# Raw weights of groups 2 to 4 land in buffers of the units, the first six state products are copied to C and A, and the list of operations is ordered anew

## The chip, the cores and the metric

The kernel runs on one core of a Trainium2 chip. The metric is the device time of one launch in microseconds. Three runs of the kernel before gave 668.93, 672.35 and 676.08 us, a median of 672.35 us. One more execution was profiled: 671.54 us, of which 669.7 us are the span from the first instruction to the last; all times of the trace count from the start of that span.

## The reference

The program is cross attention between tokens and a small state, followed by a feed-forward layer with a rational activation. The weights arrive as float64.

```python
# x [8, 8, 512, 64], state [8, 8, 32, 64]
a = softmax(scale * x @ state.T);      xread = a @ state
a2 = softmax(scale * state @ x.T);     sread = a2 @ x
x = concat([xread, sread])             # to 8 * 544 rows of 512
h = x @ w_in                           # w_in [512, 2048], float64
P = a[0] + a[1] * h + a[2] * h**2 + a[3] * h**3
Q = 1.0 + abs(b[0]) * abs(h) + abs(b[1]) * h**2
out = (P / (Q + 1e-06)) @ w_out        # w_out [2048, 512], float64
```

## The kernel before

**Tiling.** The 2048 hidden columns are cut into 8 blocks u of 256. A step n is one batch b = n // 8 and one block u = n % 8; steps 0 to 63 cover the eight batches, steps 64 to 71 the state rows. For the batches the kernel does not compute x @ w_in: it multiplies the state with w_in first (a state product), and step n then multiplies that product m with the transposed softmax aT. TensorE therefore needs, for step n, the product m of its batch and block.

**State products.** X:i (i = 4u + e, 32 of them) multiplies block u of w_in with the states of batches 2e and 2e + 1, on TensorE, into one of two PSUM buffers of two banks (tag `h`, shared with the h of the steps and with the attention of batches 1 to 7). XA:i (ScalarE) or XV:i (VectorE) copies the result out of PSUM into a tile of the tag `xo`, of which there are two; XS:i stores that tile to a scratch tensor in HBM. For batch 0 the product is not stored but split at once into a high part (fh, ScalarE) and a low part (fo, VectorE). For the later batches lm:n loads a pair of products back and fs:n splits each (ScalarE, then GpSimd).

**Weights.** 16 groups k in the order in0, in1, in2, out0, in3, out1, in4, out2, ...; each is 1 MB of float64 in two halves of 512 KB, the size of most transfers here. lr:i (i = 2k + j) loads half j of group k into a tile of the tag `raw`, which has two tiles of two halves: the halves of group k + 2 wait until group k has been read. cp:k (ScalarE) and jr:k (VectorE) take the two 32-bit words of each number apart, jl:k (VectorE) joins them to float32. An "in" group becomes a tile win of block u (three buffers), stored with jw:u for later; an "out" group is split by sp:k (ScalarE, then GpSimd) into the resident w_out.

**A step.** F:n:0 and F:n:1 (TensorE, 6 matmuls each) make h in PSUM. FC:n and FB:n (ScalarE) write C and A from it; mu, po, qd (VectorE) read h again, qa, ln, ex (ScalarE) make the reciprocal L; g1, g2, g3 (VectorE) and gl (GpSimd) or gv (VectorE) make the high and low part gh and gl. mh:n:t (4 matmuls) and ml:n:t (2 matmuls) multiply them with w_out for row block t. C and A have three buffers each, L, gh and gl two each.

**What sets the order.** A list ORDER of some 2200 tokens. Each engine, and SyncE (SP) which issues all loads and stores, executes its tokens strictly in the order in which they stand in the list; a token waits only for its data and its buffers, and everything behind it on its engine waits with it. Attention of a batch (scores, row_T, row_max, row_sub, row_exp, row_sum, row_eps, row_norm, a_T, a_hi, a_lo; col_max, col_scale, col_exp, e2_T, sread and so on) stands in the same list. Names that end in p (row_sup, a_lp) are the GpSimd form of the same operation, those in v (row_norv) the VectorE form.

The lines that the change touches are `load_raw` (L271 to L285), `conv_parts` and `join_rest` (L287 to L311), `extra_out` (L615 to L619) and ORDER.

Of the kernel before, what the change touches and what calls it, by code (L numbers as in the profile page):

```python
# [9 lines left out]
F32 = mybir.dt.float32  # L10
F32R = mybir.dt.float32r
I32 = mybir.dt.int32
U32 = mybir.dt.uint32
# [5 lines left out]
P = 128  # L19
# [169 lines left out]
def attention_rational_ffn(  # L189
# [9 lines left out]
    S = 2 * xT.shape[4]  # L199
# [744 lines left out]
```

## Time and profile before

| what | value |
|---|---|
| median of three runs | 672.35 us (668.93 to 676.08) |
| profiled execution | 671.54 us |
| its span | 669.7 us |
| TensorE (PE) busy | 643.5 us |
| VectorE (DVE) busy | 624.2 us |
| ScalarE (ACT) busy | 515.8 us |
| GpSimd (POOL) busy | 318.3 us |
| mean granted TensorE clock | 0.989 of 2.4 GHz |

Busy time is the union of an engine's instructions. The span is best read in three pieces: the first 134 us, in which the weights are loaded, converted and multiplied with the state beside the eight steps of batch 0; the 519 us of the later steps; and the last 17 us.

### The profile page before, as it was taken

How to read it: one execution, taken by the hardware profiler on the slowest of the kernel's cores; microseconds unless marked ns; L12 is line 12 of the kernel's file. 1: busy time of each engine (PE TensorE's matmuls, PEld its weight loads, DVE VectorE, ACT ScalarE, POOL GpSimd, SP SyncE). 2: the span in 40 equal slices, each digit the busy share in tenths (PEclk: the TensorE clock that was granted, in tenths of full speed). 3: DMA queues.
4: the chain of work that ended last, by engine and by line, in shares of the span. 5: the costliest groups of instructions: out<-in, count | busy, mean ns of one | idle time of the engine just before them, and what ended most of it. 6: DMA issues, size and time to landing. Idle time of an engine off the chain costs nothing.

```text
span 669.7 us, 11219 instructions
## 1 busy us (share of the span) xinstructions
PE 643.5 (96%) x4474; PEld 512.9 (77%) x4474; DVE 624.2 (93%) x593; ACT 515.8 (77%) x611; POOL 318.3 (48%) x172
## 2 busy tenths in 40 slices
PE   6769989999999999999999999999999999999997
PEld 3445556778887888788887888788878888888995
DVE  5889999999999999999999999999999899999885
ACT  4689898887877887787868787797787678865663
POOL 1105255355454566545554545555446446465541
PEclk8989999999999999999999999999999999999999
DMA  7889987615112422213223132231225101211301
GB/s 298 310 315 335 331 329 257 226 54 178 44 34 93 136 77 96 69 26 105 85 101 120 71 89 69 79 142 32 95 79 174 32 1 47 64 47 60 100 1 63
DMA packets 28984, 81.46 MB, mean 122 GB/s; under 512 B 2820, under 2 KB 2948, under 8 KB 28932
## 3 DMA queue, kind: packets, MB, share of 16 engines
q1 hardware_dynamic: 28932, 80.75, 35.1%
q8 instruction: 35, 0.57, 0.3%
q14 instruction: 17, 0.14, 0.1%
HBM read 52.95 MB, written 27.79 MB: 121 GB/s over the span
## 4 chain that ended last, share of the span: by engine, by line
PE 88%; DMA 5%; ACT 3%; DVE 2%; issue 1%; SPq 1%; ACTq 0%
PE h L696 28%; DMA m_dram<-xo 3%; PE ps_x L607 3%; PE o__5754 L769 2%; PE o__3525 L769 2%; PE o__1763 L769 2%; PE o__2310 L769 2%; PE o__4679 L769 2%; PE o__4049 L769 2%; PE o__2879 L769 2%; PE o__3495 L769 2%; PE o__5233 L769 2%; PE o__2341 L769 2%; PE o__5794 L769 2%; PE o__4054 L769 2%; PE o__5172 L769 2%
## 5 line engine op out<-in xcount | busy, mean ns | idle before, releaser
L759 POOL TENSOR_TENSOR gl<-C,L 128x1024 fp32r<-128x1024 f32 (+1 forms) x70 | 174.1, 2487 | 230.4 <-DVE C L752 174.0
L696 PE MATMUL h<-aT,m 128*128 128x512 f32 x768 | 191.3, 396 | 4.2 <-DVE xo L619 4.1
L696 PEld LDWEIGHTS h<-aT,m 128*128 128x128 f32 x768 | 144.9, 190 | 38.5 <-issue 3.5
L708 ACT ACTIVATE C<-h,cst 128x1024 f32<-128x1024 f32 (+1 forms) x72 | 83.3, 1157 | 44.6 <-PE h L696 32.1
L656 POOL TENSOR_TENSOR m<-m_sb,m 128x512 fp32r<-128x512 f32 x56 | 79.9, 1432 | 60.3 <-ACT m L655 40.0
L715 ACT ACTIVATE A<-h,cst 128x1024 f32<-128x1024 f32 (+1 forms) x72 | 76.7, 1066 | 29.2 <-PE h L696 26.9
L740 DVE SCALAR_TENSOR_TENSOR gh<-C,cst,L 128x1024 fp32r<-128x1024 f32 (+1 forms) x72 | 91.8, 1274 | 6.2 <-ACT L L811 2.6
L729 DVE SCALAR_TENSOR_TENSOR A<-A,b0a,h 128x1024 f32<-128x1024 f32 (+1 forms) x72 | 87.5, 1216 | 9.4 <-ACT A L715 7.2
L752 DVE SCALAR_TENSOR_TENSOR C<-C,cst,A 128x1024 f32<-128x1024 f32 (+1 forms) x72 | 88.8, 1233 | 2.2
L723 DVE SCALAR_TENSOR_TENSOR C<-C,cst,h 128x1024 f32<-128x1024 f32 (+1 forms) x72 | 87.8, 1219 | 2.1
L746 DVE SCALAR_TENSOR_TENSOR A<-A,gh 128x1024 f32<-128x1024 f32 (+1 forms) x72 | 88.0, 1222 | 1.6
L735 ACT ACTIVATE A<-A 128x1024 f32<-128x1024 f32 (+1 forms) x72 | 72.7, 1012 | 19.2 <-DVE A L729 19.1
L719 DVE TENSOR_TENSOR C<-C,h 128x1024 f32<-128x1024 f32 (+1 forms) x72 | 82.9, 1152 | 3.9 <-ACT C L708 2.4
L801 ACT ACTIVATE L<-A 128x1024 f32<-128x1024 f32 (+1 forms) x72 | 73.0, 1013 | 3.4 <-POOL gl L759 0.3
L811 ACT ACTIVATE L<-L 128x1024 f32<-128x1024 f32 (+1 forms) x72 | 72.9, 1014 | 1.5
L607 PE MATMUL ps_x<-win_sb,st 64*32 64x256 f32 x1024 | 36.3, 403 | 15.2 <-DVE win_sb L320 6.3
L607 PEld LDWEIGHTS ps_x<-win_sb,st 64*32 64x32 f32 x1024 | 17.8, 111 | 30.9 <-ACT xo L619 10.5
L655 ACT CAST m<-m_sb 128x512 fp32r<-128x512 f32 x56 | 33.9, 614 | 0.0
L619 ACT COPY xo<-ps_x 128x1024 f32<-128x1024 f32 (+1 forms) x26 | 23.8, 933 | 5.0 <-PE ps_x L607 2.8
L332 POOL TENSOR_TENSOR wo<-cv_r,wo 128x1024 fp32r<-128x1024 f32 x7 | 16.9, 2410 | 17.6 <-ACT wo L331 17.6
L696 PEld LDWEIGHTS h<-sh,m 128*128 128x128 f32 x192 | 24.2, 191 | 0.7
L696 PE MATMUL h<-sh,m 128*128 128x256 f32 x192 | 24.4, 283 | 0.0
(254 smaller groups left out, 1113.2 us busy)
## 6 DMA issues: line engine op xcount, KB each, us to landing
m_sb<-m_dram SPq DMA_DIRECT2D x28, 512.0 KB, 4.5
m_dram<-xo SPq DMA_DIRECT2D x24, 512.0 KB, 4.2
out_dram<-o_sb SPq DMA_DIRECT2D x34, 256.0 KB, 4.3
xT_sb<-in_xT_dram SPq DMA_DIRECT2D x16, 512.0 KB, 5.1
raw<-in_w_in_dram SPq DMA_DIRECT2D x16, 512.0 KB, 6.4
raw<-in_w_out_dram SPq DMA_DIRECT2D x16, 512.0 KB, 5.6
x_sb<-in_x_dram SPq DMA_DIRECT2D x16, 512.0 KB, 7.0
w_in_dram<-win_sb SPq DMA_DIRECT2D x8, 512.0 KB, 5.4
```

Of the source, the lines that this page charges most:

```text
L656: nc.gpsimd.tensor_tensor(m[:, 1], t, m[:, 0].bitcast(F32), op=ALU.subtract)
L696: nc.tensor.matmul(h[:, ci * W : (ci + 1) * W], l, r, start=(q == 0), stop=(q == len(seq) - 1),)
L708: nc.scalar.activation(e["C"], e["h"], AF.Identity, scale=cst[:, 3:4], bias=cst[:, 2:3])
L715: nc.scalar.activation(e["A"], e["h"], AF.Abs, scale=cst[:, 5:6])
L719: nc.vector.tensor_tensor(e["C"], e["C"], e["h"], op=ALU.mult)
L723: nc.vector.scalar_tensor_tensor(e["C"], e["C"], cst[:, 1:2], e["h"], op0=ALU.add, op1=ALU.mult)
L729: nc.vector.scalar_tensor_tensor(e["A"], e["A"], b0a, e["h"], op0=ALU.add, op1=ALU.mult)
L740: nc.vector.scalar_tensor_tensor(e["gh"], e["C"], cst[:, 0:1], e["L"], op0=ALU.add, op1=ALU.mult)
L746: nc.vector.scalar_tensor_tensor(e["A"], e["A"], 1.0 + 1e-6, e["gh"].bitcast(F32), op0=ALU.add, op1=ALU.mult)
L752: nc.vector.scalar_tensor_tensor(e["C"], e["C"], cst[:, 0:1], e["A"], op0=ALU.add, op1=ALU.subtract)
L759: eng.tensor_tensor(e["gl"], e["C"], e["L"], op=ALU.mult)
L769: nc.tensor.matmul(O[t], e[l][:, j * W + t * P : j * W + (t + 1) * P], wo[:, k, 2 * u + j, :], start=(place == FIRST[n // U, t] and i + j ...
```

## The change

Three things. First, the raw halves of groups 2, 3 and 4 (halves 4 to 9) land in tiles of the tags gl, gh and L, which no step uses yet, and not in `raw`. Second, the first six state products (X:0 to X:5) are copied to tiles of the tags C and A (three each), and not to `xo`. Third, ORDER is another list of nearly the same tokens.

```diff
+    EARLY = {2: "gl", 3: "gh", 4: "L"}
+    XEARLY = {0: "C", 1: "C", 2: "C", 3: "A", 4: "A", 5: "A"}
+    BUFS = {"C": 3, "A": 3, "L": 2, "gh": 2, "gl": 2}
+
+    def spare(tag, dtype):
+        return ew.tile([P, 2 * S], dtype, name="spare", tag=tag, bufs=BUFS[tag])
+
...
-        if i // 2 not in RAW:
-            RAW[i // 2] = cv.tile([P, 2, 2 * CW, 2], U32, name="raw", tag="raw", bufs=2)
-        r = RAW[i // 2][:, j]
+        k = i // 2
+        if k in EARLY:
+            RAW[k, j] = spare(EARLY[k], U32).rearrange("p (f w) -> p f w", w=2)
+        elif (k, 0) not in RAW:
+            t = cv.tile([P, 2, 2 * CW, 2], U32, name="raw", tag="raw", bufs=2)
+            RAW[k, 0], RAW[k, 1], RAW[k, None] = t[:, 0], t[:, 1], t
+        r = RAW[k, j]
...
-        t = XO[i] = ew.tile([P, 2, 2, CW], F32, name="xo", tag="xo", bufs=2)
+        if i in XEARLY:
+            t = spare(XEARLY[i], F32).rearrange("p (q j f) -> p q j f", q=2, j=2)
+        else:
+            t = ew.tile([P, 2, 2, CW], F32, name="xo", tag="xo", bufs=2)
+        XO[i] = t
```

Of the list, one line of each start:

```diff
-    "warm:8 lt:0:0 ls:0:2 lt:0:1 scores:0:0 lc scores:0:1 cb b0a row_T:0:0 row_max:0:0 row_sub:0:0 lr:1 "
+    "lt:0:0 warm:8 ls:0:2 scores:0:0 lt:0:1 lc lr:1 cp:0:1 lr:0 cp:0:0 scores:0:1 row_T:0:0 jr:0:1 "
```

Some tokens change their form. The conversion of groups 2, 3 and 4 (cp, jr) goes half by half. From VectorE to GpSimd go row_sub of batches 0 (first half) and 1, row_norm of batch 0 (second half) and of batch 7 (first half), and a_lo of batches 0 (first half), 1 and 7; to VectorE goes row_norm of batch 2 (second half). XV, the VectorE form of the copy, is used for products 5, 13, 16, 26, 30, 31 and no longer for 4, 5, 11, 12, 20, 27. Of the low parts of the last steps, gl:66 and gl:68 become gv and gv:69 becomes gl.

**SP, from the first weights on** (raw and spare: weights on their way in; xo and, in the change, some spare tiles to m_dram: state products on their way out; win_sb: converted blocks of w_in; x_sb: the tokens). Before:

```order
L277 DMA raw<-in_w_in_dram 128x1024 x2
L252 DMA st<-in_stT_dram 128x768
L277 DMA raw<-in_w_in_dram 128x1024 x2
L283 DMA raw<-in_w_out_dram 128x1024 x2
L624 DMA m_dram<-xo 128x512
L624 DMA m_dram<-xo 128x1024 x2
L277 DMA raw<-in_w_in_dram 128x1024 x2
L624 DMA m_dram<-xo 128x1024
L352 DMA x_sb<-in_x_dram 128x1024
L624 DMA m_dram<-xo 128x1024
L277 DMA raw<-in_w_in_dram 128x1024
```

With the change:

```order
L288 DMA raw<-in_w_in_dram 128x1024 x4
L253 DMA st<-in_stT_dram 128x768
L288 DMA spare<-in_w_in_dram 128x1024
L294 DMA spare<-in_w_out_dram 128x1024 x2
L288 DMA spare<-in_w_in_dram 128x1024
L644 DMA m_dram<-spare 128x1024 x2
L288 DMA spare<-in_w_in_dram 128x1024 x2
L644 DMA m_dram<-spare 128x512
L341 DMA w_in_dram<-win_sb 128x1024
L644 DMA m_dram<-spare 128x1024
L294 DMA raw<-in_w_out_dram 128x1024 x2
L288 DMA raw<-in_w_in_dram 128x1024
```

Eight weight halves now stand ahead of the first product store, where four stood whose buffers were free and two that waited for one; the loads of x_sb stand later, behind further stores.

**VectorE, from the copy of X:5 to the first elementwise operations of step 0 and 1** (L619 or L639: the copies XV; L304 or L320 and the line after: jr and jl of a group; L636 or L656: fo; L719, L723, L729 or L739, L743, L749: mu, po, qd). Before:

```order
L619 COPY xo<-ps_x 128x2x2x256
L304 TENSOR_SCALAR cv_r<-raw 128x1024
L320 SCALAR_TENSOR_TENSOR cv_r<-cv_y,cv_r 128x1024
L636 TENSOR_TENSOR m<-ps_x,m 128x512
L475 TENSOR_SCALAR r_217<-r_217 128x2
L619 COPY xo<-ps_x 128x512
L304 TENSOR_SCALAR cv_r<-raw 128x1024
L320 SCALAR_TENSOR_TENSOR win_sb<-cv_y,cv_r 128x1024
L719 TENSOR_TENSOR C<-C,h 128x1024
L729 SCALAR_TENSOR_TENSOR A<-A,b0a,h 128x1024
L723 SCALAR_TENSOR_TENSOR C<-C,cst,h 128x1024
L729 SCALAR_TENSOR_TENSOR A<-A,b0a,h 128x1024
```

With the change:

```order
L639 COPY spare<-ps_x 128x2x2x256
L442 TENSOR_SCALAR cm<-cm 128x1 x2
L320 TENSOR_SCALAR cv_r<-spare 128x512 x2
L336 SCALAR_TENSOR_TENSOR win_sb<-cv_y,cv_r 128x1024
L320 TENSOR_SCALAR cv_r<-spare 128x512
L656 TENSOR_TENSOR m<-ps_x,m 128x512
L320 TENSOR_SCALAR cv_r<-spare 128x512
L749 SCALAR_TENSOR_TENSOR A<-A,b0a,h 128x1024
L320 TENSOR_SCALAR cv_r<-spare 128x512
L336 SCALAR_TENSOR_TENSOR cv_r<-cv_y,cv_r 128x1024
L739 TENSOR_TENSOR C<-C,h 128x1024
L743 SCALAR_TENSOR_TENSOR C<-C,cst,h 128x1024
```

The second copy of this stretch (XV:4) has left VectorE, group 2 is joined ahead of group 3, and the halves of group 3 fill the places between the operations of step 0.

## Rows read from the trace of the kernel before

**Rows 1.** The page, busy time of each engine, its share of the span, and its instructions.

```profile
PE 643.5 (96%) x4474; PEld 512.9 (77%) x4474; DVE 624.2 (93%) x593; ACT 515.8 (77%) x611; POOL 318.3 (48%) x172
```

**Rows 2.** Stretches of the span: from:to and length in us, busy us of each engine with its instructions, then the granted TensorE clock, the share of DMA time that was busy, and GB/s moved.

```profile
0.00:16.75 16.75, 10.46 (x138) 6.37 (x146) 8.93 (x17) 7.88 (x15) 2.80 (x8) 0.80 0.80 298
16.75:33.50 16.75, 11.78 (x152) 7.81 (x136) 13.79 (x21) 11.51 (x16) 3.28 (x2) 0.91 0.90 310
33.50:50.25 16.75, 11.32 (x212) 7.62 (x211) 14.26 (x16) 14.26 (x18) 1.40 (x2) 0.88 0.90 316
50.25:67.00 16.75, 15.25 (x204) 9.96 (x203) 15.34 (x14) 15.69 (x18) 9.28 (x4) 1.00 0.91 337
67.00:83.75 16.75, 15.68 (x245) 9.74 (x251) 15.62 (x17) 13.82 (x16) 3.33 (x2) 1.00 0.92 329
...
134.00:653.00 519.00, 519.00 (x2910) 427.73 (x2909) 498.03 (x452) 401.43 (x470) 272.24 (x145) 1.00 0.24 77
```

**Rows 3.** The chain that ended last, in order of time, from 0 to 140 us: start, length, what the chain went through. A DMA piece runs from its issue to its landing.

```profile
21.27 7.37 DMA m_dram<-xo
...
31.36 7.62 DMA m_dram<-xo
...
109.45 8.74 DMA x_sb<-in_x_dram
```

**Rows 4.** SP in order of time: start, length (of the issuing), line, what is moved.

```profile
4.39 0.94 SPq L277 DMA_DIRECT2D raw<-in_w_in_dram  x2
10.51 0.80 SPq L283 DMA_DIRECT2D raw<-in_w_out_dram  x2
...
19.10 1.15 SPq L277 DMA_DIRECT2D raw<-in_w_in_dram  x2
```

**Rows 5.** VectorE in order of time: start, length, line and operation; in brackets the idle time before it and what ended it.

```profile
7.60 0.72 DVE L441 STREAM_TRANSPOSE e<-ps_sc__109 128x512 f32<-128x512 f32 x1 [6.62 <-PE ps_sc__110 L402]
8.35 0.69 DVE L458 TENSOR_REDUCE mx<-e 128x16 f32<-128x512 f32 x1
9.07 0.69 DVE L466 TENSOR_TENSOR e<-e,mx 128x512 f32<-128x512 f32 x1
9.68 0.76 DVE L304 TENSOR_SCALAR cv_r<-raw 128x512 int32<-128x512 uint32 x2
10.56 1.23 DVE L320 SCALAR_TENSOR_TENSOR win_sb<-cv_y,cv_r 128x1024 int32<-128x1024 int32 x1
...
17.66 1.23 DVE L320 SCALAR_TENSOR_TENSOR win_sb<-cv_y,cv_r 128x1024 int32<-128x1024 int32 x1
...
22.31 1.21 DVE L619 COPY xo<-ps_x 128x1024 f32<-128x1024 f32 x1
...
28.67 0.69 DVE L619 COPY xo<-ps_x 128x512 f32<-128x512 f32 x1 [2.30 <-DMA m_dram<-xo]
...
33.53 1.28 DVE L723 SCALAR_TENSOR_TENSOR C<-C,cst,h 128x1024 f32<-128x1024 f32 x1
...
51.42 1.28 DVE L729 SCALAR_TENSOR_TENSOR A<-A,b0a,h 128x1024 f32<-128x1024 f32 x1 [1.75 <-ACT C L708]
```

**Rows 6.** TensorE in order of time, in the same columns. Each F of a step is one row x12 (steps 0, 1, 2, 3, 5 and 9 here), each X one row x32, each mh one row x4.

```profile
11.84 3.67 PE L607 MATMUL ps_x<-win_sb,st 64*32 64x256 f32 x64 [4.01 <-DVE win_sb L320]
...
23.57 3.04 PE L696 MATMUL h<-aT,m 128*128 128x512 f32 x12 [1.18 <-DVE xo L619]
29.51 4.49 PE L696 MATMUL h<-aT,m 128*128 128x512 f32 x12 [2.90 <-DVE xo L619]
34.95 1.10 PE L607 MATMUL ps_x<-win_sb,st 64*32 64x256 f32 x32 [0.95 <-DVE C L723]
...
44.76 4.37 PE L696 MATMUL h<-aT,m 128*128 128x512 f32 x12
48.97 1.07 PE L769 MATMUL o__573<-wo,gh 128*128 128x512 f32 x4
49.88 1.07 PE L769 MATMUL o__580<-wo,gh 128*128 128x512 f32 x4
50.88 1.09 PE L607 MATMUL ps_x<-win_sb,st 64*32 64x256 f32 x32
51.91 1.20 PE L769 MATMUL o__621<-wo,gh 128*128 128x512 f32 x4
...
58.32 3.03 PE L696 MATMUL h<-aT,m 128*128 128x512 f32 x12
...
91.38 3.01 PE L696 MATMUL h<-aT,m 128*128 128x512 f32 x12
...
134.79 2.88 PE L696 MATMUL h<-aT,m 128*128 128x512 f32 x12
```

**Rows 7.** GpSimd in order of time, in the same columns: row_sub and a_lo of a half of batch 0.

```profile
15.03 1.05 POOL L466 TENSOR_TENSOR e<-e,mx 128x512 f32<-128x512 f32 x1 [0.17 <-DVE mx L458]
22.54 1.27 POOL L522 TENSOR_TENSOR aT<-eT,aT 128x512 fp32r<-128x512 f32 x1 [6.46 <-ACT aT L518]
```

**Rows 8.** Groups of instructions of the first 140 us, shapes apart: line, engine, operation, shapes and count; busy us, mean ns of one; idle before them in us, and what ended it. XA of a whole product, cp of half a group, FC.

```profile
L619 ACT COPY xo<-ps_x 128x1024 f32<-128x1024 f32 x21 | 20.8, 1015 | 2.6 <-DMA m_dram<-xo 1.3 <-PE ps_x L607 0.8 <-ACT cv_y L294 0.4
...
L708 ACT ACTIVATE C<-h,cst 128x1024 f32<-128x1024 f32 x10 | 12.1, 1206 | 3.5 <-PE h L696 3.4
...
L294 ACT ACTIVATE cv_y<-raw 128x512 f32<-128x512 f32 x4 | 2.7, 673 | 0.7 <-DMA raw<-in_w_in_dram 0.6
```

More of the change, by code (lines that the diff above doesn't have):

```diff
@@ L263, in attention_rational_ffn @@
             groups.append(("in", u + 3))
-    NU = 2 * len(groups)
+    EARLY = {2: "gl", 3: "gh", 4: "L"}
[3 more added lines that the diff above has]
+        return ew.tile([P, 2 * S], dtype, name="spare", tag=tag, bufs=BUFS[tag])
     RAW, CV, win_t = {}, {}, {}
@@ L285, in load_raw, with raw_words @@
             )
+    def raw_words(k, j, w):
+        if j is None:
+            return RAW[k, None][:, :, :, w]
+        return RAW[k, j][:, :, w].unsqueeze(1)
     def conv_parts(k, j=None):
@@ L295, in conv_parts @@
             CV[k][0][:, js].bitcast(F32),
-            RAW[k][:, js, :, 1].bitcast(F32),
+            raw_words(k, j, 1).bitcast(F32),
             AF.Prelu,
@@ L305, in join_rest @@
             CV[k][1][:, js],
-            RAW[k][:, js, :, 0],
+            raw_words(k, j, 0),
             2.0**-29,
```

319 rows, old and new, of the table ORDER are left out of this document.

## The prediction, on record before the change was run

> **What bounds the kernel now.** I read the busy shares first: TensorE is busy 96% of the span, VectorE 93%, ScalarE 77%, GpSimd 48% [rows 1]. An average over stages says little, so I cut the span [rows 2]. Between 134 and 653 us TensorE is busy 519.00 of 519 us: there TensorE's own work sets the time, and an order can only lose. In the first 50.25 us it is busy 33.6 us, in the next 33.5 us 30.9. What the change can win lies there. In the same stretches the DMA engines are busy 0.80 to 0.92 of the time and VectorE, after the first, 13.8 to 15.6 of 16.75 us: three resources are near their limits.
>
> Then I asked how late TensorE is. One instruction of a product or a step has a fixed price on a busy TensorE: 4 matmuls of mh 0.91 us (from 48.97 to 49.88), one product X 1.03 us (from 50.88 to 51.91), so 0.227 us a matmul [rows 6]. With these I add up all TensorE work that stands ahead of F of a step in the list, and call the start of F minus that sum the time lost so far. Ahead of step 3 stand 14 products (14.4 us), 36 matmuls of F (8.2), 14 of mh and ml (3.2), and 6.4 us of warming, scores, transposes and sread: 32.2 us, and F of step 3 starts at 58.32, so 26.1 us are lost. In the same way: 12.1 us at step 0 (23.57), 15.3 at step 1 (29.51), 22.8 at step 2 (44.76), 29.8 at step 5 (91.38), 33.0 at step 9 (134.79) [rows 6]. The remaining 530 us lose 4.3 more, and 4.7 us pass after the last matmul (copy out and store). So four fifths of the loss is made before step 3.
>
> Why, the chain in order of time tells [rows 3]: 7.37 us from the issue of a product store at 21.27 to its landing, and 7.62 us from another at 31.36. A copy out of PSUM waits for one of two xo tiles, that tile waits for its store, and the store stands in the DMA queue behind weight loads. The copy at 28.67 shows it: idle 2.30 us, ended by that DMA [rows 5], and F of step 1 had waited 2.90 us for this copy [rows 6]. Further, SP has four weight halves under way at 5.3 us and issues the next two at 10.51 and two more at 19.10, when `raw` tiles come free and product stores ahead of them have gone [rows 4].
>
> **The change part by part, as a walk along the new order.** Durations are those of before; landings are worked out from bytes. In the first stretch the trace moves 298 GB/s at a busy share of 0.80, later 337 at 0.91: 0.37 MB per us when busy [rows 2].
>
> *Until 18 us nothing is won.* VectorE starts at 7.60, when the scores exist, as before [rows 5]. Ahead of the first join stand two transposes, two halves of jr and two maxima, 3.5 us, instead of 2.9: the join ends at 12.2, before at 11.7. The second join ends at about 18.3 instead of 18.8 [rows 5].
>
> *Raw halves in gl, gh and L.* They cost no instruction. SP issues them directly behind the first four, by 7 us. With 2.2 MB ahead of groups 1 and 2 and 0.52 MB each they land at 13, 15, 16.5 and 18 us, before their cp and jr are reached. The buffers are free again long before use: gh of step 0 is written at about 36 us. Six halves of cp cost 0.67 us each against 1.2 for a whole group [rows 8], 0.2 us more a group on ScalarE, hidden where it waits for h.
>
> *The six products in C and A.* Copies 0 to 5 no longer wait for stores. I follow them: X:1 at 16.1 (after the low part of step 0 has read its bank), X:2 at 17.2, X:5 at 18.4, X:4 at 19.8, each 1.03 us, each behind a copy of 0.9 to 1.2 us of the product two before. F of step 0 needs the bank of X:5, read by VectorE until 20.8: it starts at 20.9 instead of 23.57, with 10.6 us of work ahead instead of 11.5, so 10.3 lost. F of step 1 needs the low part of product 4, at 24.0: 24.3 instead of 29.51, 10.5 lost. The new wait is that C and A can't be written by step 0 before the stores have read them. FC:0 comes at 26.1; the store of X:0 is issued at about 19.6 with some 1.6 MB ahead of it, so it lands at 25 to 26. Bounds for this wait: 0, and 2.2 us if it takes the 8.7 us of the slowest piece in the chain [rows 3]. I take 0, since 1.6 MB and its own 0.26 MB at the rate above end at 24.6; behind FC:0 stand all VectorE operations of step 0, so it would cost its full length.
>
> *Steps 2 and 3.* Now VectorE leads: qd, mu, po of steps 0 and 1 with the jr and jl of groups 3, 4 and 5 between them (1.2 us each for the large ones, 0.7 for jr) run without a gap from 25 to 39 us. The next products wait for po of step 0, which ends at 30.2 (before 34.8 [rows 5]) and for po of step 1 at 33.8. F of step 2 then starts at 37.4 instead of 44.76, qd of step 2 at 43.1 instead of 51.42 [rows 5], although VectorE has 34.1 us of work ahead instead of 35.9. Product 13, two pieces of mh and ml, sread (its tokens land at about 46) and products 7, 10 and 11 bring F of step 3 to 50.0, with 31.5 us of work ahead: 18.5 us lost instead of 26.1, **a gain of 7.6 us**.
>
> *From step 3 on.* Before, 6.9 us are lost from step 3 to 9, and 4.3 later. VectorE gives up 4.9 us of work by the moved operations (row_sub 0.69 there and 1.05 on GpSimd, a_lo 1.27 there [rows 5, 7]); GpSimd, at 48%, takes them. I cost this at 0: bounds are a gain of 4.9, if VectorE alone led up to step 9, and a loss of 1.4 (two halves at 1.05 and 1.27 instead of 0.69 and 0.65) where the new place lies on the way to aT. One new wait I price: the first reload of products, lm:8, stands directly behind the store of product 27, 4 us of TensorE work ahead of its use; before, 8 us. A store and a reload take some 4 us alone and up to 8.7 in the full queue; I put 1 us, between 0 and 4.7. The end of the list has the same work after the last F (48 matmuls, 10.9 us), and its VectorE chain stays ahead: 0.
>
> Sum: 671.5 of the profiled execution, less 7.6, plus 1.0: 664.9, say **665 us**. The median of the runs shown is 0.8 us above that execution; I leave the number as it is.
>
> **A rule against it.** Ahead of F of step 5 the new list has 28.8 MB to move (counted in it, at 0.52 MB a half, a product or a reload, 0.26 MB where half a product is stored). At 0.37 MB per us, which the rows give [rows 2], that takes until 79 us, and my walk puts step 5 at 84: the queue keeps up if it hardly ever idles. The Trainium skill (DMA: Bandwidth & Descriptors, the table at its head) gives some 358 GB/s as the HBM limit of one core, by which the same bytes would take until 82 us. The stretches of this trace, 298 to 337 GB/s with their idle time, lie below that figure.
>
> **The rivals.**
> *The DMA queue was the bound, and stays it.* The same weights, products and tokens go through it. At the mean rate of the first five stretches, 318 GB/s [rows 2], 28.8 MB pass at 90.6 us, against 91.38 for step 5 before: what step 3 wins is given back by waits of the copies and of cp, and 0.8 us remain, 670.7 us. For it: a busy share of 0.9 already. Against: the idle tenth comes from SP waiting for tiles, which this change removes early; weights are prefetched by several us; and about 1 MB less stands ahead of the same TensorE work. Half of it would leave 668.
> *The new order makes TensorE wait in the long stretch, and the kernel gets slower.* There it never idles now [rows 2]. A wait of 0.25 us in each of the 56 steps is 14 us: 678 us with the gain. It decides from 0.25 us a step; at 0.12 it eats the gain. For it: all places are new, and GpSimd takes over operations 1.5 times as long. Against: I compared, step by step, the TensorE work ahead of the first mh with the VectorE work ahead of g1; the new list leaves VectorE 2 to 5 us more room in nearly all steps, and its reloads stand at least 5.7 us ahead from step 9 on.
> *The buffers in C, A, L, gh and gl hold step 0 up.* The landing of a store from C or A decides: at 26 us it is free, at 34 us it eats the whole gain (671.5), and only past 40 us is it slower by 1%. Nothing in the chain took that long.
>
> **How the numbers follow.** The gain kept as walked: 0.52. The queue takes half or all of it back (668 to 671), or the buffers do: 0.38. Slower by stalls in the long stretch: 0.10. The likeliest gives 665. Its own bounds are 660 (VectorE's 4.9 us also won) and 669 (lm:8 at its worst, 4.7 us). The range reaches to the rival of the queue: 659.5 to 671.5. A measurement of this kernel can tell about 1% (6.7 us) from no change; 665 is 1.1% under the median, so much of my likeliest case lies close to that line: faster 0.52, same 0.38, slower 0.10.
>
> **What would show it.** Right: no copy of the first six products waits for a DMA of m_dram; F of steps 0, 1, 2 and 3 starts near 21, 24, 37 and 50 us; the busy DMA share up to 84 us is 0.95 or more; TensorE is still busy 519 of 519 us later. Wrong: F of step 3 after 55 us (a wait I missed, first of all FC:0 on a store); step 3 early but step 5 at 90 (the queue); idle TensorE after step 9, at lm:8 or later.

## The result: slower by 1.1%, and the profile after

| | before | changed |
|---|---|---|
| median of all runs (us) | 672.59 | 679.32 (676.69 to 682.06, 6 runs) |
| ratio to before, 95% interval | | 1.0113 [1.0079, 1.0146] |
| profiled execution (us) | 671.54 | 678.48 |
| its span (us) | 669.7 | 676.7 |

The forecast was 665 us, range 659.5 to 671.5. The time lies above the range, and the sign is the other one.

The page after, busy time of each engine (answers to [rows 1]):

```profile
PE 650.5 (96%) x4474; PEld 513.6 (76%) x4474; DVE 627.3 (93%) x590; ACT 516.1 (76%) x615; POOL 324.1 (48%) x177
```

TensorE has the same 4474 instructions and is busy 7.0 us longer: just the difference of the spans. The stretches (answer to [rows 2], same columns):

```profile
0.00:16.75 16.75, 9.33 (x130) 5.92 (x138) 9.03 (x18) 8.57 (x15) 5.94 (x10) 0.73 0.86 340
16.75:33.50 16.75, 12.05 (x180) 7.69 (x172) 14.02 (x21) 14.34 (x21) 3.25 (x2) 0.91 0.90 321
33.50:50.25 16.75, 14.99 (x249) 9.13 (x235) 15.09 (x15) 14.31 (x20) 6.11 (x3) 0.75 0.87 313
50.25:67.00 16.75, 14.38 (x165) 9.72 (x165) 13.13 (x15) 12.56 (x16) 5.86 (x3) 0.90 0.85 294
67.00:83.75 16.75, 16.58 (x260) 11.19 (x264) 16.57 (x17) 15.97 (x19) 5.46 (x3) 1.00 0.88 315
134.00:660.00 526.00, 525.33 (x2917) 429.33 (x2916) 502.17 (x452) 402.34 (x472) 271.11 (x145) 1.00 0.23 77
```

In the last row TensorE is busy 525.33 of 526.00 us, nearly all the time, as it was before (519.00 of 519 us). A busy share does not say that the same work takes the same time. TensorE in order of time (answers to [rows 6]; the x17 and x15 are one product in two pieces):

```profile
21.83 3.05 PE L716 MATMUL h<-aT,m 128*128 128x512 f32 x12
26.33 3.04 PE L716 MATMUL h<-aT,m 128*128 128x512 f32 x12 [1.01 <-DVE m L656]
32.42 1.96 PE L623 MATMUL ps_x<-win_sb,st 64*32 64x256 f32 x32 [3.05 <-DVE C L743]
36.06 5.38 PE L623 MATMUL ps_x<-win_sb,st 64*32 64x256 f32 x96 [1.68 <-DVE C L743]
41.37 3.31 PE L716 MATMUL h<-aT,m 128*128 128x512 f32 x12
...
52.92 0.83 PE L623 MATMUL ps_x<-win_sb,st 64*32 64x256 f32 x17 [0.79 <-ACT xo L639]
55.34 0.94 PE L623 MATMUL ps_x<-win_sb,st 64*32 64x256 f32 x15 [1.58 <-issue]
56.21 2.93 PE L716 MATMUL h<-aT,m 128*128 128x512 f32 x6
...
134.93 1.64 PE L716 MATMUL h<-aT,m 128*128 128x512 f32 x6
...
605.60 1.55 PE L716 MATMUL h<-aT,m 128*128 128x512 f32 x6
```

F of steps 0, 1, 2 and 3 starts at 21.83, 26.33, 41.37 and 56.21 us (forecast 20.9, 24.3, 37.4, 50.0). The time lost so far, worked out as in the prediction (start of F less the price of the TensorE work ahead of it), puts the 7.0 us in their places:

| lost, us | up to step 3 | 3 to 9 | 9 to 63 | after 63 |
|---|---|---|---|---|
| before | 26.1 | 6.9 | 3.8 | |
| changed | 24.7 | 9.8 | 8.9 | |
| difference | -1.4 | +2.9 | +5.1 | +0.4 |
| forecast | -7.6 | +1.0 | 0 | 0 |

Three things to explain: a start-up that won 1.4 us instead of 7.6, a middle that gave it back twice over, and a long stretch, fully busy, that takes 5.1 us more.

### The profile page after: what moved, and what is told of

Its sections match the earlier page's. It is cut to its first block, busy times and chain, and to the rows that moved or that the text cites. A ratio compares the mean times of both kernels' runs of the same rounds, so it can differ in the third digit from the quotient of the medians.

```text
span 676.7 us, 11201 instructions
## 1 busy us (share of the span) xinstructions
PE 650.5 (96%) x4474; PEld 513.6 (76%) x4474; DVE 627.3 (93%) x590; ACT 516.1 (76%) x615; POOL 324.1 (48%) x177
## 3 DMA queue, kind: packets, MB, share of 16 engines
HBM read 52.95 MB, written 27.79 MB: 119 GB/s over the span
## 4 chain that ended last, share of the span: by engine, by line
PE 80%; DVE 7%; ACT 4%; DMA 4%; issue 2%; POOL 1%; SPq 0%; DVEq 0%; ACTq 0%; POOLq 0%
PE h L716 27%; PE o__2328 L789 2%; PE ps_x L623 2%; PE o__2337 L789 2%; PE o__5754 L789 2%; PE o__3456 L789 2%; PE o__4105 L789 2%; PE o__4704 L789 2%; PE o__2939 L789 2%; PE o__5240 L789 2%; PE o__5188 L789 2%; PE o__5761 L789 2%; PE o__5213 L789 2%; PE o__4696 L789 2%; PE o__3482 L789 2%
## 5 line engine op out<-in xcount | busy, mean ns | idle before, releaser
L779 POOL TENSOR_TENSOR gl<-C,L 128x1024 fp32r<-128x1024 f32 (+1 forms) x69 | 171.3, 2483 | 263.7 <-DVE C L772 190.2
L716 PE MATMUL h<-aT,m 128*128 128x512 f32 x768 | 194.4, 399 | 2.5 <-DVE m L656 1.0
L735 ACT ACTIVATE A<-h,cst 128x1024 f32<-128x1024 f32 (+1 forms) x72 | 76.4, 1064 | 33.8 <-PE h L716 29.5
L760 DVE SCALAR_TENSOR_TENSOR gh<-C,cst,L 128x1024 fp32r<-128x1024 f32 (+1 forms) x72 | 94.1, 1307 | 4.9 <-PE o__2328 L789 1.9
L749 DVE SCALAR_TENSOR_TENSOR A<-A,b0a,h 128x1024 f32<-128x1024 f32 (+1 forms) x72 | 87.4, 1215 | 10.1 <-ACT A L735 8.3
L743 DVE SCALAR_TENSOR_TENSOR C<-C,cst,h 128x1024 f32<-128x1024 f32 (+1 forms) x72 | 87.6, 1218 | 2.0
L676 POOL TENSOR_TENSOR m<-m_sb,m 128x512 fp32r<-128x512 f32 x56 | 74.9, 1345 | 28.6 <-ACT m L675 23.1
L739 DVE TENSOR_TENSOR C<-C,h 128x1024 f32<-128x1024 f32 (+1 forms) x72 | 83.1, 1154 | 3.6 <-ACT C L728 2.0
L623 PE MATMUL ps_x<-win_sb,st 64*32 64x256 f32 x1024 | 39.4, 438 | 14.8 <-DVE C L743 6.5
L623 PEld LDWEIGHTS ps_x<-win_sb,st 64*32 64x32 f32 x1024 | 19.6, 119 | 31.5 <-issue 15.5
L675 ACT CAST m<-m_sb 128x512 fp32r<-128x512 f32 x56 | 33.8, 615 | 10.7 <-PE h L716 6.3
L716 PE MATMUL h<-sh,m 128*128 128x256 f32 x192 | 24.2, 284 | 0.0
L639 ACT COPY xo<-ps_x 128x1024 f32<-128x1024 f32 (+1 forms) x21 | 19.0, 913 | 5.8 <-PE ps_x L623 3.7
```

The source lines that it names most:

```text
L676: nc.gpsimd.tensor_tensor(m[:, 1], t, m[:, 0].bitcast(F32), op=ALU.subtract)
L716: nc.tensor.matmul(h[:, ci * W : (ci + 1) * W], l, r, start=(q == 0), stop=(q == len(seq) - 1),)
L735: nc.scalar.activation(e["A"], e["h"], AF.Abs, scale=cst[:, 5:6])
L739: nc.vector.tensor_tensor(e["C"], e["C"], e["h"], op=ALU.mult)
L743: nc.vector.scalar_tensor_tensor(e["C"], e["C"], cst[:, 1:2], e["h"], op0=ALU.add, op1=ALU.mult)
L749: nc.vector.scalar_tensor_tensor(e["A"], e["A"], b0a, e["h"], op0=ALU.add, op1=ALU.mult)
```

## The experiments

Runs go by the first part of their labels. Times are medians; ratios are to the kernel before, run beside each, with 95% intervals; "lost" is the time lost up to F of steps 3, 9 and 63, in the one profiled execution of each kernel. "F" is the mean distance from start to start of the F matmuls of steps 9 to 63.

| run | us | ratio | F, ns | lost at 3 / 9 / 63 |
|---|---|---|---|---|
| before | 672.59 | 1 | 227 | 26.1 / 33.0 / 36.8 |
| changed | 679.32 | 1.0113 [1.0079, 1.0146] | 232 | 24.7 / 34.5 / 43.4 |
| a1 | 676.08 | 1.0072 [1.0045, 1.0099] | 227 | 24.1 / 32.2 / 37.5 |
| a2 | 676.98 | 1.0075 [1.0057, 1.0093] | 232 | 26.5 / 33.8 / 41.9 |
| a3 | 670.76 | 0.9980 [0.9963, 0.9997] | 227 | 25.6 / 33.4 / 37.5 |
| a5 | 675.79 | 1.0065 [1.0043, 1.0087] | 227 | 24.1 / 33.7 / 39.1 |
| b1 | 671.97 | 1.0008 [0.9986, 1.0030] | 227 | 25.4 / 32.3 / 36.2 |
| b2 | 675.58 | 1.0065 [1.0042, 1.0088] | 232 | 24.8 / 31.9 / 39.9 |
| b3 (one run) | 676.00 | | 233 | 25.0 / 33.0 / 41.7 |
| g128 (one run) | 669.83 | | 227 | 23.6 / 31.1 / 35.1 |
| f1 | 675.67 | 1.0070 [1.0040, 1.0101] | 227 | 24.5 / 34.9 / 40.1 |
| c1 | 674.57 | 1.0044 [1.0019, 1.0069] | 227 | 25.9 / 35.9 / 40.2 |
| c2 | 676.45 | 1.0074 [1.0050, 1.0098] | 227 | 24.2 / 31.1 / 41.0 |
| d1 | 675.45 | 1.0056 [1.0035, 1.0076] | 227 | 24.4 / 35.1 / 40.5 |
| d2 (one run) | 672.92 | | 227 | 23.6 / 31.3 / 37.8 |
| d3 | 671.99 | 0.9999 [0.9982, 1.0017] | 227 | 21.5 / 30.4 / 35.7 |
| d4 | 669.78 | 0.9971 [0.9957, 0.9986] | 227 | 20.8 / 30.9 / 35.0 |
| h1 | 674.07 | 1.0037 [1.0022, 1.0052] | 227 | 21.3 / 32.7 / 36.8 |
| h2 | 677.30 | 1.0076 [1.0054, 1.0099] | 227 | 21.6 / 39.1 / 43.2 |
| h3 | 672.21 | 1.0019 [1.0000, 1.0039] | 227 | 21.0 / 33.5 / 37.6 |

### The long stretch: where tiles lie

In the changed kernel the medians by position of a matmul in F are 234, 229, 237, 229, 237, 229 ns; before, all six are 227. A pool gives addresses to its tags in the order of first use, and the new order uses them first in another order: aT went from byte 47968 of a partition to 43744 (addresses as in the built programs). The theory of places says that this makes the matmuls slow; its rival, the theory of order, that it is what other engines do at the time. The edit allots tiles that nothing uses, tag by tag (their shapes are left out here). All later kernels but a2 and the b's, f1 and g128 have every tag at its old address.

```diff
+    def pin(pool, tags):
+        for tag, shape, bufs in tags:
+            for _ in range(bufs):
+                pool.tile(shape, F32, name="pin_" + tag, tag=tag, bufs=bufs)
+    pin(at, [e1, mx, sT, cm, rs, e2T, e2, r2, aT, sr])   # order of before
+    pin(ew, [xo, m, A, C, L, gh, gl])
```

> The changed kernel, order and buffers as they are, with one difference: tiles without any instruction are allotted at the start of the pools, tag by tag, so that every tag of the pools at and ew lies at the address that it has in the kernel before (aT at byte 47968 of a partition instead of 43744, m at 106336 instead of 110432, and so on). Theory of places: the two-in-three slow start-to-start distances of the F matmuls (medians 234, 229, 237, 229, 237, 229 ns in the six positions, against 227 in all six before) come from where tiles lie: here all six are 227 ns again and the time is about 679.3 - 768 x 5.4 ns = 675.2 us (674 to 676.5). Theory of order: they come from what other engines do at the time under the new order: medians stay at 234/229/237 and the time at 679.3 +- 1.

> The kernel before, order and buffers as they are, with the pool at laid out as in the changed kernel (aT at byte 43744, e2 at 60192, the small tiles moved with them); the pool ew is left where it was, m included. Theory of places, with aT as the tile that counts: F matmuls at 234, 229, 237, 229, 237, 229 ns and the time at 672.6 + 4.2 = 676.8 us (675.5 to 678). Theory of places with m as the tile that counts, or theory of order: 227 ns and 672.6 +- 1.

a1 has 227 ns, a2 the slow pattern: a2 differs from the kernel before in nothing but places, and is slower by 0.75% (5.0 us). So the theory of order has fallen for these matmuls. The next question is which property of the place counts.

> The kernel before, order and buffers as they are, with the pool at laid out so that aT lies at byte 43872 of a partition: 128 bytes above its place in the changed kernel (43744) and 4096 below that in the kernel before (47968). If it counts how the address stands to a grid of 256 bytes (43872 and 47968 leave 96, 43744 leaves 224): F matmuls at 227 ns and the time as the kernel before, 671.5 +- 1. If it counts in which region of the memory aT lies, or which tiles lie beside it: F at 234/229/237 ns and 676 to 678.

> The kernel before with aT at byte 47840: 128 bytes below its old place, e2 and the others ahead of it as before but for the two small tiles cm and r2, which lie behind it. If the grid of 256 bytes counts (47840 leaves 224): F matmuls at 234, 229, 237, 229, 237, 229 ns and 676 to 678 us. If the region counts: 227 ns and 671.5 +- 1.

```diff
-    pin(at, [e1, mx, sT, cm, rs, e2T, e2, r2, aT, sr])   # aT at 47968
+    pin(at, [e1, sT, mx, rs, e2T, cm, r2, aT, e2, sr])   # b1, f1: 43872
+    pin(at, [e1, sT, mx, rs, e2T, e2, aT, cm, r2, sr])   # b2: 47840
+    pin(at, [e1, mx, sT, cm, rs, e2T, e2, aT, r2, sr])   # b3: 47904
+    at.tile([P, 32], F32, name="pad", tag="pad")         # g128, ahead of the first pin
```

128 bytes decide it, and not the region: b1, close to the new place, is fast, b2, close to the old one, slow by 0.65%.

> The changed kernel with one difference: the two small tiles cm and r2 (64 bytes each) are allotted ahead of aT instead of behind it, so that aT lies at byte 43872 instead of 43744; e2 and the small tiles move by up to 16 KB within the same stretch, everything else stays. If the address of aT is the whole of the slow F matmuls here: 227 ns in all six positions and the time as a1, 675 to 676.5, 0.4 to 0.7 per cent under the changed kernel. If other places that a1 also put back count: 230 to 233 ns on average, 677 to 679.

> The kernel before with a tile of 128 bytes that nothing uses at the head of the pool at, so that all tiles behind it lie 128 bytes higher: aT at 48096 and m, gh, gl, wo too leave 224 above a multiple of 256. If an operand's own address counts: F matmuls at 234/229/237 ns and, wo being the moving operand there, the matmuls of the second product (mh, ml) slower than 227 ns as well, 10 to 25 us in all. If it counts how the two operands stand to each other: everything at 227 ns and the time as before, 670 to 674. If only aT's own address counts and wo's does not: F slow, mh and ml at 227, 676 to 678.

> The kernel before with aT at byte 47904, 64 below its old place (32 above a multiple of 256; m stays at 96). If the half of the 256-byte grid counts (32 and 96 lie in the lower half, 224 in the upper): 227 ns and 670 to 674 us. If every offset between aT and m other than 0 is slow: 230 ns or more and 674 to 678.

f1 is the changed kernel with that one address mended: 227 ns, and the same time as a1, so aT accounts for all that places cost here. g128 and b3 settle which property: with every tile moved by 128 bytes nothing is slow, with aT alone moved by 64 all six positions are. TensorE around 400 us, whole steps and the row behind each, in the kernel before, g128, b3, and the changed kernel:

```profile
409.32 2.88 PE L696 MATMUL h<-aT,m 128*128 128x512 f32 x12
412.04 0.62 PE L769 MATMUL o__3514<-wo,gl 128*128 128x512 f32 x2
```

```profile
410.31 0.62 PE L778 MATMUL o__3547<-wo,gl 128*128 128x512 f32 x2
413.03 2.88 PE L705 MATMUL h<-aT,m 128*128 128x512 f32 x12
415.75 1.07 PE L778 MATMUL o__3528<-wo,gh 128*128 128x512 f32 x4
```

```profile
412.27 2.96 PE L703 MATMUL h<-aT,m 128*128 128x512 f32 x12
415.07 0.62 PE L776 MATMUL o__3530<-wo,gl 128*128 128x512 f32 x2
```

```profile
406.46 2.94 PE L716 MATMUL h<-aT,m 128*128 128x512 f32 x12
409.24 1.09 PE L789 MATMUL o__3527<-wo,gh 128*128 128x512 f32 x4
```

From the start of F to the next row pass 2.72, 2.72, 2.80 and 2.78 us for 12 matmuls. Over a multiple of 256 bytes aT and m leave 96 and 96 (before, b1, f1) and 224 and 224 (g128): fast; 224 and 96 (changed, a2, b2) and 32 and 96 (b3): slow. So aT's own address is not the cause (g128), but how aT stands to something that g128 moved along with it. That this is m, the stationary operand of the same matmul, is the plain reading and not a tested one: m alone was not moved. Why the hardware does so is open, and other distances than 0, 64 and 128 were not tried.

### What is left: the new order's start and rest

> The order of the kernel before with the buffers of the changed one, all at the old addresses: raw groups 2 and 3 land in gl and gh (group 4 stays in the two buffers of raw, because in the old order the first logarithm asks for L before group 4 is read), the first six products are copied to C and A; cp and jr of groups 2 and 3 are split in halves. If the buffers alone bring the start-up's gain: F of step 3 starts 2 to 5 us before 58.3 and the time is 668 to 671. If the gain needs the new order, because the products' stores and the conversions still follow each other on SP and ACT: F of step 3 within 1 us of 58.3 and the time 672 +- 1.2.

```diff
-EARLY = {2: "gl", 3: "gh", 4: "L"}     # a3, with the old ORDER, cp and jr of groups 2, 3 halved
+EARLY = {2: "gl", 3: "gh"}
-XS:3 jr:2:1 XS:1 jl:2 lr:9 cp:4:1 jr:4:1 FB:0 fo:1 lr:8     # a5
+lr:9 lr:8 XS:3 jr:2:1 XS:1 jl:2 cp:4:1 jr:4:1 FB:0 fo:1
```

> a1_old_places with one more edit: the loads of raw group 4 (lr:9, lr:8) are issued ahead of the stores of products 3 and 1, which wait for ACT on SP until 17.1 and 19.3 us. If that wait is what made F of step 1 late (ACT and VectorE waited for this transfer until 25.2 us): F of step 1 starts about 1.2 us earlier than in a1, F of step 3 too, and the time is 1.0 to 1.5 us below a1. Rival: the wait only covers for VectorE and ACT, which are full from 21 us on: F of step 3 within 0.4 us of a1 and the time within 0.5 us.

a3: the buffers alone, in the old order, bring 0.2%, and F of step 3 at 57.9: nearly the second case of its expectation. a5 (lr:9 and lr:8 ahead of XS:3 and XS:1) moves F of step 1 from 26.3 to 25.2 us as expected, but step 3 and the time stay, as in the rival case. The rival's reason is not what the traces show: F of step 2 comes 1.1 us earlier too (40.08 instead of 41.15), and is then held up by a halt of TensorE (below) that ends at 55.00 us in a1 and in a5.

c1 and c2 join two orders: the tokens of one up to F:9:1, then all tokens of the other that are left.

> All tiles at the old addresses. The new order and all new buffers up to the last F of step 9 (about 135 us), then what is left in the order of the kernel before. If the new order costs its 4 to 5 us (a1 is 1.0072 of before, its twin with the old order 0.998) in the long stretch, as by the 1.0 us gap ahead of an F at 184 us and its neighbours: as a3, 670 to 671.5 us. If it costs them in the start-up: as a1, 675 to 676. Half and half: 673.

> The mirror of c1, at the old addresses: the order of the kernel before up to the last F of step 9, with raw groups 2 and 3 in gl and gh and six products in C and A (as a3), then what is left in the new order. If the new order costs in the long stretch: 675 to 676 us. If in the start-up: 670 to 671.5.

c1 lies between its cases. By lost time the rest (9 to 63) costs 4.3 us in the old order (c1; 4.1 in a3) and 5.2 to 5.4 in the new (a1, a5, f1): the new rest costs 1.2 us, 0.66 us of it in a single wait, in the changed kernel ahead of 187.46 us:

```profile
187.46 1.87 PE L716 MATMUL h<-aT,m 128*128 128x512 f32 x7 [0.66 <-DVE C L743]
```

c2 is inconclusive: its seam alone loses 3.1 us (two gaps at 139 and 144 us). The new start stands at 32.2 to 35.9 us at step 9 (changed, a1, a5, c1, f1), the old at 31.1 to 33.8 (before, a2, a3, b1, b2, c2). Two of its losses have one place in the trace each.

**A held VectorE.** VectorE and GpSimd in the changed kernel, then VectorE and GpSimd in d1, in order of time:

```profile
110.07 1.28 DVE L772 SCALAR_TENSOR_TENSOR C<-C,cst,A 128x1024 f32<-128x1024 f32 x1
111.27 2.37 DVE L491 TENSOR_SCALAR r<-r 128x2 f32<-128x2 f32 x1
113.67 0.17 DVE L495 RECIPROCAL r<-r 128x2 f32<-128x2 f32 x1
```

```profile
111.01 2.59 POOL L348 TENSOR_TENSOR wo<-cv_r,wo 128x1024 fp32r<-128x1024 f32 x1 [6.93 <-ACT wo L347]
```

```profile
79.43 3.47 DVE L777 SCALAR_TENSOR_TENSOR C<-C,cst,A 128x1024 f32<-128x1024 f32 x1
...
109.98 0.16 DVE L496 TENSOR_SCALAR r<-r 128x2 f32<-128x2 f32 x1
```

```profile
79.43 2.40 POOL L353 TENSOR_TENSOR wo<-cv_r,wo 128x1024 fp32r<-128x1024 f32 x1 [4.38 <-ACT wo L352]
```

In the changed kernel a step on 2 columns (col_eps:1) lasts 2.37 us and ends with GpSimd's split of w_out (113.60). d1 puts it, with col_norm:1, ahead of g2:5:

```diff
-g2:5 g3:5 col_eps:1 col_norm:1 fh:7 fo:7
+col_eps:1 col_norm:1 g2:5 g3:5 fh:7 fo:7
```

> a5_raw4_before_stores with one more edit: the two small VectorE steps col_eps and col_norm of batch 1 (128x2 elements) stand ahead of second and third of step 5 instead of behind them. In a1, a5, c1 and the changed kernel the first of them lasted 2.37 us instead of 0.17, from 0.1 to 0.3 us after the start of GpSimd's 2.5 us split of w_out (sp:13) to its end. If VectorE was held by GpSimd there, and is what sets F of step 7: the step lasts 0.2 us, F of step 7 comes 1.5 to 2.2 us earlier for the same F of step 6, the lost time from step 6 to step 7 falls from 4.2 us (a5) to about 2, and the time falls to 673.5 to 674.3. Rival: a DMA or another wait is next, F of step 7 does not move and the time stays at 675.8.

The step lasts 0.16 us, and the loss from step 6 to 7 falls from 4.2 to 2.6 us. But the median falls by only 0.3 us, well inside the intervals: the hold is shown, its worth in time is not. In d1's execution another step, at 79.43, lasted 3.47 us instead of 1.28; it starts together with a GpSimd split (79.43 to 81.83). Which step meets a split differs from one trace to another. The Trainium skill (Trainium Architecture — The Big Picture, What this means for kernel authors) says that VectorE and GpSimd share a port pair of the memory under an exclusive lock; these rows agree, with 2.2 us as the price of one meeting. The traces also show that it matters which of the two begins first: in the changed kernel the 36 full-size steps of g1, g2 and g3 that begin while a GpSimd step runs last 1.56 us on average and up to 3.32, while the 158 others, 15 of which see a GpSimd step begin during them, last 1.26 us and none over 1.29.

**A halt within a product.** Product 11 stops behind its 17th matmul (the rows at 52.92 and 55.34 above), on nothing that semaphores show, in the changed kernel, a1, a5, c1, d1 and f1; no kernel with the old start has a halt within a product. d2 is d1 with four more matmuls, which are 8 rows of the trace, in the warm-up at the very start:

```diff
-warm:8
+warm:12
```

> d1_eps_moved with four more pairs of matmuls in the warm-up at the very start (8 more matmul rows ahead of everything else, in a stretch where TensorE waits for its first data anyway). In all kernels with the new start, product 11 halts behind its 17th matmul for 1.9 to 3.5 us on nothing that the profile shows, just after a 16 KB transfer of the instruction queue has begun; no kernel with the old start does. If TensorE there waits for a block of its own instructions, the place moves with the count of instructions: the halt comes behind the 9th matmul of product 11, and lasts about as long. If it is something of product 11 itself (its data, its buffer, a shared port): still behind the 17th.

TensorE in d2, and the line of the changed kernel's page on queue 8, the instruction queue (number of transfers, MB, share):

```profile
51.20 0.64 PE L628 MATMUL ps_x<-win_sb,st 64*32 64x256 f32 x9 [0.31 <-ACT xo L644]
54.12 1.06 PE L628 MATMUL ps_x<-win_sb,st 64*32 64x256 f32 x23 [2.27 <-issue]
```

```profile
q8 instruction: 35, 0.57, 0.4%
```

The halt has moved to behind the 9th, by the 8 matmuls added 50 us earlier: TensorE waits for its own instructions. The queue has 35 transfers of 16 KB in the whole run, and TensorE has 4474 matmuls and as many weight loads, some 256 for each transfer. One of them begins at 52.95 in the changed kernel (resumed 55.34), 53.96 in c1 (56.33), 51.82 in d2 (54.12): 2.2 to 2.4 us before TensorE goes on, in all seven halts (these six kernels and d2). The Trainium skill (Runtime: NRT & Kernel Launch, Instruction fetch mechanics) says that instructions come in blocks of 16 KiB, 256 of them, and that crossing into the next is mostly hidden. The blocks agree (8 matmuls and 8 weight loads moved the halt by 8 matmuls); here, behind 64 matmuls of sread and two and a half products that use up a block in some 4 us, it costs 1.3 to 3.1 us of idle time. In the changed kernel, a5, c1 and d1 the granted clock was at 0.50 (1.2 GHz) behind the halt, and the first six matmuls of F of step 3 took 2.6 to 2.9 us; in a1, f1 and d2 it was at 1.00 and they took 1.7.

d3 moves product 11 behind F of step 3, so that 12 long matmuls stand where its 32 short ones stood:

```diff
-X:11 XA:10 F:3:0 col_norm:0 sr_copy:0 lr:15 cp:7 sr_T:0 sr_fin:0 g1:1 g2:1 XS:7 F:3:1 XA:11
+XA:10 F:3:0 col_norm:0 sr_copy:0 lr:15 cp:7 sr_T:0 sr_fin:0 g1:1 g2:1 XS:7 F:3:1 X:11 XA:11
```

> d1_eps_moved with product 11 (X:11) behind F of step 3 instead of ahead of it. If the halt is due to instructions used up faster than their blocks come, because 64 small matmuls of sread and three products of 32 stand one behind the other: with 12 F matmuls of 227 ns in the place of product 11 the block is there in time, no halt over 0.4 us, F of step 3 starts 3 us earlier than in d1 (1.0 the product, 2 the halt), lost time at step 3 about 2 us less. How much of it is left at step 7 depends on VectorE: if it is full from 67 us on, under 1 us; time 673 to 674 then, 671.5 to 672.5 if all of it is kept.

> d3_x11_later up to the last F of step 9, then what is left in the old order, as c1. If the account is right (new rest costs 1.2 us of TensorE more than the old, the halt 2, VectorE's hold 2): 1 to 1.5 us below d3, about 671 to 672, no slower than the kernel before and perhaps 0.1 % faster. If the start-up of the new order is slow for another reason still: 673 to 675.

TensorE in d3:

```profile
49.68 1.96 PE L628 MATMUL ps_x<-win_sb,st 64*32 64x256 f32 x64
51.95 1.68 PE L721 MATMUL h<-aT,m 128*128 128x512 f32 x6 [0.31 <-ACT xo L644]
```

d3 has no halt. F of step 3 starts at 51.95 instead of 55.89, 1.03 us of that because product 11 no longer stands ahead of it; 3.5 us of the median are gone against d1, and it is level with the kernel before. In d1 the halt was 1.74 us and the low clock behind it cost 1.0 more (2.68 against 1.68 us for six matmuls of F); the rest of the 3.5 us has no row of its own. In d3 a transfer of the queue begins at 51.77 us too, and no gap in TensorE's rows follows it; what sets its start is open. d4 adds the old rest and is 0.3% faster than the kernel before: F of step 3 at 51.3, step 9 at 131.4. It is the fastest of the kernels with more than one run.

**What takes back a gain of step 3.** d4 is 5.3 us ahead of the kernel before at step 3, 2.1 at step 9, 1.8 at the end. Work added between them says what binds:

```diff
+            if i in (16, 17, 20, 21):               # h1
+                nc.sync.dma_start(
+                    extra32[i % 8].bitcast(U32), w_in[u, j].rearrange("p c f -> p (c f)")
+                )
...
         for name, args in tokens:
             ops[name](*args)
+            if name == "jr" and 8 <= args[0] <= 15:  # h2
+            if name == "cp" and 8 <= args[0] <= 12:  # h3
+                ops[name](*args)
```

> d4_new_start_mended_old_rest with four more transfers of 0.52 MB (raw halves 16, 17, 20 and 21 are each copied once more, to memory that nothing reads, directly behind their load), between about 55 and 90 us: 2.1 MB, 5.7 us of the queue at 0.37 MB per us. If the queue binds between step 3 and step 9: F of step 9 and the time 4 to 6 us later. If it has room (it is busy 0.81 to 0.92 there): under 1.5 us.

> d4 with the step jr of weight groups 8 to 15 done twice on VectorE (the same result written again): 8 times 0.69 us, 5.5 us of VectorE work between about 60 and 125 us. If VectorE binds there: F of step 9 and the time 4 to 5.5 us later. If it has room: under 1.5 us.

> d4 with the step cp of weight groups 8 to 12 done twice on ScalarE: 5 times 1.16 us, 5.8 us of ScalarE work between about 60 and 105 us. If ScalarE binds, because copies out of PSUM, cp and the activations of the steps stand in one queue: 4 to 6 us later. If it has room (13.8 to 15.5 us of 16.75 busy): under 1.5 us.

Against d4 (difference of the ratios, times 671.5 us; each good to some 2 us): VectorE's 5.5 us cost 7.1, the queue's 5.7 cost 4.4, ScalarE's 5.8 cost 3.2. VectorE binds first; none has much room, and the queue and ScalarE are not told apart. Why 5.5 us cost 7.1 is open; the granted clock, 0.92 from 83.75 to 100.50 us in h2 and 1.00 in d4, may be a part of it. VectorE in h2 (third column of busy times):

```profile
67.00:83.75 16.75, 13.52 (x183) 9.29 (x189) 16.58 (x15) 13.28 (x16) 7.78 (x3) 0.97 0.89 303
83.75:100.50 16.75, 14.96 (x168) 9.50 (x150) 16.54 (x14) 12.69 (x14) 5.01 (x3) 0.92 0.66 221
100.50:117.25 16.75, 13.49 (x170) 8.98 (x171) 16.51 (x20) 11.36 (x15) 7.53 (x5) 1.00 0.70 245
```

## Why the prediction was wrong, step by step

- **Until 18 us, and the copies.** Right. The joins end at 12.2 and 18.5 (12.2 and 18.3 forecast), F of step 0 starts at 21.83 (20.9), and none of the first six copies waits for a store.
- **Raw halves "by 7 us".** True of four of six. Group 4 is issued at 19.70, behind two stores, and ScalarE waited for it until 25.17. Worth 1.1 us at F of steps 1 and 2, nothing at step 3 behind the halt, and nothing in the time (a5).
- **Steps 2 and 3, "a gain of 7.6 us".** This step failed: 1.4 measured. F of step 3 came 6.2 us behind its place in the walk (56.21 for 50.0), in three parts of some 2 us each. First a wait that was walked too early: FC:0 came at 28.20 (26.1) behind three halves of cp, not behind a store, and po of step 0 ended at 32.28 (30.2). Then the clock, for which the walk had no term: the three products at 36.06 took 5.38 us instead of the 3.1 that I had put, because the granted clock was 0.50, that is 1.2 GHz, from 32.4 to 41.4 us, after TensorE had stood idle 3.05 us. Last the halt, 1.58 us in the changed kernel and 1.3 to 3.1 in all: no term of the walk was for instructions. With product 11 moved (d3, d4), the time lost at step 3 is 20.8 to 21.5, not 18.5; the three products still take 4.9 to 5.0 us there.
- **From step 3 on, "0".** Failed twice. Up to step 9 I took the gain as kept, where VectorE, the queue and ScalarE each have little room (h1 to h3): of 5.3 us at step 3, 2.1 stay in d4. And I wrote that in the long stretch "an order can only lose" and looked for waits alone. 3.6 of the 5.1 us there are slower matmuls (660 matmuls of F by 5.5 ns), from an address that neither order nor diff names.
- **The rivals.** Slower by stalls in the long stretch, with 678 us, came nearest in time and not in cause: waits of the new rest make up 1.2 of the 5.1 us. The queue that takes the gain back has part of the truth, between steps 3 and 9. The buffers did not hold step 0 up.
- **lm:8.** Put at 1 us; lost time rises by 0.2 from step 7 to 8.
- **The signs.** "F of step 3 after 55 us" came about (56.21). The busy share of the queue up to 84 us was 0.85 to 0.90, not 0.95, and TensorE was busy all the time later, as I had asked for as a sign of being right: that sign cannot see a slower matmul. The rate of a full queue was put too low: d4 moved 382 GB/s from 16.75 to 33.50 us, more than the 0.37 MB per us of the walk and more than the limit of the rule against it.
- **What stays open.** From the changed kernel to d4 the ratio falls from 1.0113 to 0.9971, which is 9.5 us: 2.9 by the address (f1; a2 makes it 5.0), 0.9 from f1 to d1, 3.8 by product 11 (d3), 1.9 by the old rest (d4), each good to 2 or 3 us. Kernels with the unmended new start spread more (672.6 to 680.3 in a1, 668.7 to 671.5 in d4). The low clock behind the halt, there in some executions and not in others, may be a part of that; why the same program differs by 7 us between executions was not found.

## What to carry to other kernels

After any edit that changes which tile is allocated first, compare the addresses of matmul operands before and after, and the start-to-start distance of the same matmul in both traces: a busy share of 100% hides a slower matmul. In a start-up that three resources nearly fill, price a gain at one step by what still reaches the end (here 2 of 5 us), leave room in the sum for TensorE's lower clock behind a wait (2.3 us for three products here), and look for runs of many small matmuls, which can outrun their own instructions.

## What the runs showed of the hardware

- F32R matmuls of 128x128 by 512 columns take 227 ns each when the two operands' addresses leave the same remainder by 256 bytes (96/96, 224/224), 232 to 233 ns on average when they differ by 64 or 128 (b2, b3, a2, the changed kernel).
- TensorE can run out of instructions: it went on 2.2 to 2.4 us after a 16 KB transfer of the instruction queue had begun, in seven executions, and four more matmuls at the start moved the halt by their 8 rows (d2).
- A VectorE step that begins with or during a GpSimd step can be held to its end: 2.37 us for 128x2 elements, 3.47 us instead of 1.28 for 128x1024. One that began first was not held (15 in the changed kernel, none over 1.29 us).
- The granted clock was 0.50 for 9 us after an idle time of 3.05 us (the changed kernel, 32.4 to 41.4 us), and three products took 5.38 us there; one takes 1.03 us at 1.00.
